# Another order for emptying two accumulator banks: VectorE leads with the first bank, ScalarE copies two parts instead of three

## The chip, the cores and the metric

The kernel runs on one core of one Trainium2 chip. The metric is the device time of one execution in microseconds; the time before is the median of three runs. A profiled execution comes with it: a trace of every instruction on the engines TensorE (PE), VectorE (DVE), ScalarE (ACT), GpSimd (POOL) and SyncE (SP).

## The reference

```python
# attention with a polynomial sketch, then an MLP with exact GELU
def phi(x):                       # x: (4, 4, 1088, 32)
    a = einsum('rd,bhsd->bhsr', S1, x)
    b = einsum('rd,bhsd->bhsr', S2, x)
    return einsum('bhsi,bhsj->bhsij', a, b).reshape(..., 64)
q_p, k_p = phi(q), phi(k)
kv = einsum('bhsf,bhsd->bhfd', k_p, v);  z = sum(k_p, axis=2)
attn = einsum('bhsf,bhfd->bhsd', q_p, kv) / (einsum('bhsf,bhf->bhs', q_p, z)[..., None] + 1e-6)
x = attn.transpose(0, 2, 1, 3).reshape(4352, 128)
h = x @ w_in                      # (4352, 2048)
g = 0.5 * h * (1 + erf(h / sqrt(2)))
out = g @ w_out                   # (4352, 128)
```

The second matrix product of the MLP, `g @ w_out`, is what the change touches, or rather the step that takes its results out of the accumulators.

## The kernel before

**Tiling.** The 4352 tokens are handled in nine chunks: n = 0 to 7 have 512 tokens each, n = 8 holds the 256 that are left over. `d_ff` = 2048 is cut into 16 slices of 128 (`fi`). One step of the main loop (line 1083) is one pair (n, fi): `hidden` (line 677) makes a 128x512 tile of h in a PSUM bank on TensorE (line 683), and ScalarE turns it into g with GELU (line 690).

**The second product in seven.** For chunks 2 to 7, and for the upper half of the slices of chunks 0 and 1, `g @ w_out` is done by a scheme of the Strassen kind: a 2x2 split of tokens, slices and output channels, with seven products in place of eight. GpSimd forms the sums of g (`token_sums`, lines 732 to 735), and of the weights (`channel_sums`). `two_products` (line 754, the matmul is line 767) issues the seven products two at a time, each in a 64-row half of one of two PSUM banks. `acc[n]` is the pair of banks (a0, a1) of chunk n. They come from the pool `ops`, which has two buffers, so a chunk takes over the very two banks of the chunk ahead of it. The table `PLACE` (line 706) says where each product lies: 1, 2, 3 and 5 in bank 0 (a0), 4, 6 and 7 in bank 1 (a1). The first products of a chunk are 4 and 7 (so they need a1), then 6; 1 and 5 follow (they need a0). The last products of a chunk are 2 and 3, in a0.

**The drain.** When the last product of a chunk is issued, the loop calls `drain(n)` (line 772), ahead of the next call of `hidden`. It takes the two banks out of PSUM into two tiles of SBUF, C and N, and forms on the way the partial sums of the scheme. Its lines:

- L779, L780, L781, all on ScalarE: copies of a1's upper half (64 rows x 512), of a quarter of a1 (64x256) and of a quarter of a0 (64x256, lower half, first columns, into N).
- L783 on VectorE: a1's lower half plus the copy of L779 (64x512). It is the last read of a1.
- L785 twice, L786, L787, L788 on VectorE: five additions of 64x256, each with one operand from a0. L788 adds the two column halves of a0's lower half: one of them from PSUM, the other from the copy that L781 made. It is the last read of a0.

Later `store(n)` combines C and N (lines 801 to 804), transposes (line 829) and writes the chunk out by SP's DMA queue (line 838 or 841).

**What sets the order.** Each engine runs its instructions in the order of the program text (lines 1133 to 1139 tie it down). Waits between engines are semaphores that the framework derives from the tiles that are read and written. The banks of the next chunk are free for TensorE once the last read of each is over.

Of the kernel before, what the change touches and what calls it, by code (L numbers as in the profile page):

```python
# [16 lines left out]
def kernel(  # L17
# [18 lines left out]
    pe, dve, act, pool, sp = nc.tensor, nc.vector, nc.scalar, nc.gpsimd, nc.sync  # L36
# [735 lines left out]
    def drain(n):  # L772


        C, N = (att.tile([128, 2, CW], FP, name="sums") for i in range(2))
        lo, hi, one, two = slice(0, 64), slice(64, 128), slice(0, HW), slice(HW, CW)
        a0, a1 = acc[n]

        act.copy(out=C[lo, 0], in_=a1[hi])  # L779
        act.copy(out=N[hi, 0, one], in_=a1[hi, one])  # L780
        act.copy(out=N[lo, 0, one], in_=a0[lo, one])  # L781

        dve.tensor_add(out=C[lo, 1], in0=a1[lo], in1=C[lo, 0])  # L783
        for half in (lo, hi):
            dve.tensor_add(out=C[half, 0, one], in0=a0[lo, one], in1=C[lo, 1, two])  # L785
        dve.tensor_add(out=C[hi, 0, two], in0=a0[hi, two], in1=C[hi, 0, one])  # L786
        dve.tensor_add(out=N[hi, 1, one], in0=a0[hi, one], in1=C[hi, 0, two])  # L787
        dve.tensor_add(out=N[lo, 1, one], in0=a0[lo, two], in1=N[lo, 0, one])  # L788
        drained[n] = C, N

    usual = {}
# [291 lines left out]
    for t in range(len(steps) + LAG):  # L1083
# [29 lines left out]
        for n in drains[t]:  # L1113
            drain(n)
# [55 lines left out]
```

## Time and profile before

| | us |
|---|---|
| median of three runs | 263.39 (263.13 to 263.56) |
| the profiled execution, its own time | 263.46 |
| its span, from first to last instruction | 261.7 |
| TensorE busy in the span | 256.7 |
| VectorE busy | 150.7 |
| ScalarE busy | 116.6 |
| GpSimd busy | 164.0 |

The granted TensorE clock is 1.000 over the span. "Chain of work" below means the chain that ended last, followed back from the last instruction; its list gives the start, the length and the kind of each piece. In the timeline a line gives start, duration, engine, source line, operation, output and input tiles, and in square brackets how long the engine sat idle ahead of it and what ended that. A matmul of fp32 data shows up as two entries of the trace; 64-column matmuls run two side by side, so two entries can carry the same start. The ends of matmuls are modelled.

There are eight drains (n = 0 to 7). Their L779 start at 67.11, 81.63, 109.79, 137.50, 166.41, 193.68, 221.31 and 245.83 us.

### The profile page before, as it was taken

How to read it: one execution, taken by the hardware profiler on the slowest of the kernel's cores; microseconds unless marked ns; L12 is line 12 of the kernel's file. 1: busy time of each engine (PE TensorE's matmuls, PEld its weight loads, DVE VectorE, ACT ScalarE, POOL GpSimd, SP SyncE). 2: the span in 40 equal slices, each digit the busy share in tenths (PEclk: the TensorE clock that was granted, in tenths of full speed). 3: DMA queues.
4: the chain of work that ended last, by engine and by line, in shares of the span. 5: the costliest groups of instructions: out<-in, count | busy, mean ns of one | idle time of the engine just before them, and what ended most of it. 6: DMA issues, size and time to landing. Idle time of an engine off the chain costs nothing.

```text
span 261.7 us, 5752 instructions
## 1 busy us (share of the span) xinstructions
PE 256.7 (98%) x2331; PEld 132.7 (51%) x2331; DVE 150.7 (58%) x307; ACT 116.6 (45%) x227; POOL 164.0 (63%) x173
## 2 busy tenths in 40 slices
PE   8999999999999999999999999999999999999994
PEld 6845444344444454444444454454444444445794
DVE  2885879969697997590267948450646042600240
ACT  4674767532635334533335334533362335334441
POOL 3403007799968767687758766967778676877200
PEclk9999999999999999999999999999999999999999
DMA  6469848831000101002000020010000100010020
GB/s 200 139 200 357 164 107 206 214 81 15 3 0 15 28 4 30 10 3 40 3 0 3 0 33 11 3 30 10 3 0 14 30 4 0 14 28 0 3 40 20
DMA packets 29530, 13.48 MB, mean 52 GB/s; under 512 B 21824, under 2 KB 27712, under 8 KB 29504
## 3 DMA queue, kind: packets, MB, share of 16 engines
q1 hardware_dynamic: 29472, 13.12, 20.5%
q8 instruction: 18, 0.29, 0.5%
q14 instruction: 8, 0.07, 0.1%
q10 hardware_dynamic: 32, 0.00, 0.0%
HBM read 10.88 MB, written 2.23 MB: 50 GB/s over the span
## 4 chain that ended last, share of the span: by engine, by line
PE 96%; DVE 1%; ACT 1%; issue 0%; DVEq 0%
PE h_ps L683 44%; PE o_ps L767 33%; PE o_ps L818 5%; PE w_ps L815 3%; PE w_ps L428 1%; PE w_ps L617 1%; PE w_ps L568 1%; PE w_ps L848 1%; PE h_ps L697 1%; PE o_ps L417 1%; PE h_ps L333 1%; PE w_ps L934 1%; PE w_ps L635 0%; PE w_ps L534 0%; DVE x_tok L656 0%
## 5 line engine op out<-in xcount | busy, mean ns | idle before, releaser
L683 PE MATMUL h_ps<-xT,w_in 128*64 128x512 f32 (+3 forms) x514 | 137.3, 576 | 0.0
L690 ACT ACTIVATE block<-h_ps 128x512 f32<-128x512 f32 (+1 forms) x128 | 73.0, 570 | 120.4 <-PE h_ps L683 114.6
L767 PE MATMUL o_ps<-block,w_out 128*64 128x256 f32 x224 | 57.9, 381 | 0.3 <-DVE sums L788 0.3
L683 PEld LDWEIGHTS h_ps<-xT,w_in 128*64 128x64 f32 (+1 forms) x514 | 41.8, 143 | 29.5 <-issue 11.6
L732 POOL TENSOR_TENSOR bits_low<-block 128x512 f32<-128x512 f32 x28 | 35.6, 1273 | 28.7 <-ACT block L690 28.7
L767 PEld LDWEIGHTS o_ps<-block,w_out 128*64 128x64 f32 x224 | 30.1, 137 | 39.3 <-issue 25.3
L733 POOL TENSOR_TENSOR bits_a<-block 128x512 f32<-128x512 f32 x28 | 35.7, 1276 | 13.4 <-ACT block L690 13.4
L734 POOL TENSOR_TENSOR bits_e<-bits_a,block 128x512 f32<-128x512 f32 x28 | 36.3, 1298 | 2.2
L735 POOL TENSOR_TENSOR bits_m<-block,bits_e 128x512 f32<-128x512 f32 x28 | 35.8, 1279 | 2.2
L767 PE MATMUL o_ps<-bits_low,small 128*64 128x256 f32 x112 | 29.3, 384 | 0.0
L767 PE MATMUL o_ps<-block,small 128*64 128x256 f32 x112 | 29.3, 384 | 0.0
L767 PE MATMUL o_ps<-bits_a,small 128*64 128x256 f32 x112 | 29.1, 383 | 0.0
L783 DVE TENSOR_TENSOR sums<-o_ps,sums 64x512 f32<-64x512 f32 x8 | 5.5, 682 | 41.1 <-ACT sums L780 23.6
L767 PE MATMUL o_ps<-bits_m,w_out 128*64 128x256 f32 x112 | 28.8, 380 | 0.0
L580 DVE STREAM_TRANSPOSE w_ps<-w_ps 128x512 f32<-128x512 f32 (+1 forms) x7 | 4.8, 691 | 38.8 <-PE w_ps L568 27.8
L767 PEld LDWEIGHTS o_ps<-block,small 128*64 128x64 f32 x112 | 14.5, 137 | 18.8 <-issue 9.1
L767 PE MATMUL o_ps<-bits_e,small 128*64 128x256 f32 x112 | 17.2, 385 | 0.0
L818 PE MATMUL o_ps<-g,w_out 128*128 128x512 f32 x32 | 16.4, 598 | 0.0
L767 PEld LDWEIGHTS o_ps<-bits_m,w_out 128*64 128x64 f32 x112 | 15.4, 137 | 0.0
L767 PEld LDWEIGHTS o_ps<-bits_a,small 128*64 128x64 f32 x112 | 14.7, 137 | 0.0
L767 PEld LDWEIGHTS o_ps<-bits_low,small 128*64 128x64 f32 x112 | 14.6, 137 | 0.0
L767 PEld LDWEIGHTS o_ps<-bits_e,small 128*64 128x64 f32 x112 | 7.5, 137 | 10.5 <-issue 9.1
(181 smaller groups left out, 300.6 us busy)
## 6 DMA issues: line engine op xcount, KB each, us to landing
out_dram<-oT SPq DMA_DIRECT2D x26, 64.0 KB, 2.2
block<-in_moe_w_in_dram SPq DMA_DIRECT2D x3, 512.0 KB, 7.4
block<-in_moe_w_out_dram SPq DMA_DIRECT2D x3, 512.0 KB, 12.7
k<-in_k_dram SPq DMA_DIRECT2D x12, 128.0 KB, 3.2
v<-in_v_dram SPq DMA_DIRECT2D x12, 128.0 KB, 3.4
q<-in_q_dram SPq DMA_DIRECT2D x24, 64.0 KB, 2.3
k<-in_k_dram SPq DMA_DIRECT2D x2, 256.0 KB, 2.9
q<-in_q_dram SPq DMA_DIRECT2D x2, 256.0 KB, 4.4
```

The source lines that it names most:

```text
L333: pe.transpose(ps[:, i * 128:(i + 1) * 128], in_=s, identity=ident)
L580: dve.transpose(out=tok, in_=ps[:, :, :H2])
L683: pe.matmul(ps[rows, :W], lhsT=w[:, rows], rhs=xT[n][:, :W], start=True, stop=True)
L690: act.activation(out=g_of[n, fi][:, :W], in_=ps[:, :W], func=ACT.Gelu)
L732: pool.tensor_sub(out=s[3], in0=a11, in1=a21)
L733: pool.tensor_add(out=s[1], in0=a21, in1=a22)
L734: pool.tensor_sub(out=s[2], in0=s[1], in1=a11)
L735: pool.tensor_sub(out=s[4], in0=a12, in1=s[2])
L767: pe.matmul(acc[n][bank][half * 64:(half + 1) * 64, col:col + HW], lhsT=fixed, rhs=moving, start=opens and e == 0 and name in "4715", stop ...
L783: dve.tensor_add(out=C[lo, 1], in0=a1[lo], in1=C[lo, 0])
L815: pe.matmul(o_of[n][i][:, :128], lhsT=g[:, i * 128:(i + 1) * 128], rhs=w_tile(w_out_sb, fi), start=first, stop=final)
L818: pe.matmul(o_of[n], lhsT=w_tile(w_out_sb, fi), rhs=g, start=first, stop=final)
```

## The change

The copy of a0's quarter (L781) goes from ScalarE to VectorE and to the head of VectorE's part of the drain; the addition that uses it (L788) goes from the tail of VectorE's part to the place right behind the copy. The other lines keep their order. ScalarE's part is L779 and L780 alone.

```diff
         act.copy(out=C[lo, 0], in_=a1[hi])
         act.copy(out=N[hi, 0, one], in_=a1[hi, one])
-        act.copy(out=N[lo, 0, one], in_=a0[lo, one])
-
+
+        dve.tensor_copy(out=N[lo, 0, one], in_=a0[lo, one])
+        dve.tensor_add(out=N[lo, 1, one], in0=a0[lo, two], in1=N[lo, 0, one])
         dve.tensor_add(out=C[lo, 1], in0=a1[lo], in1=C[lo, 0])
         for half in (lo, hi):
             dve.tensor_add(out=C[half, 0, one], in0=a0[lo, one], in1=C[lo, 1, two])
         dve.tensor_add(out=C[hi, 0, two], in0=a0[hi, two], in1=C[hi, 0, one])
         dve.tensor_add(out=N[hi, 1, one], in0=a0[hi, one], in1=C[hi, 0, two])
-        dve.tensor_add(out=N[lo, 1, one], in0=a0[lo, two], in1=N[lo, 0, one])
         drained[n] = C, N
```

## The prediction

> **What bounds the kernel now.** I read the page's busy times first, then the chain of work that ended last, then its pieces around one drain, then the timeline there, and last the list of waits. The page says that TensorE is the bound:
>
> ```profile
> PE 256.7 (98%) x2331; PEld 132.7 (51%) x2331; DVE 150.7 (58%) x307; ACT 116.6 (45%) x227; POOL 164.0 (63%) x173
> ...
> PE 96%; DVE 1%; ACT 1%; issue 0%; DVEq 0%
> ```
>
> The reader is to see that the chain is TensorE for 96%: another engine's time counts only where TensorE waits for it. The pieces of the chain around the drain of chunk 2 show that it does, a little, twice:
>
> ```profile
> 109.04 0.86 PE o_ps L767 x8
> 109.90 1.72 PE h_ps L683 x8
> 111.62 1.43 PE o_ps L767 x12
> 113.05 0.86 PE h_ps L683 x4
> 113.91 1.01 PE o_ps L767 x8
> ```
>
> Eight entries of L767 take 0.86 when nothing is in their way, so twelve should take 1.29. The piece at 111.62 has 1.43 (0.14 too much), the one at 113.91 has 1.01 (0.15 too much). The timeline of the same drain says why:
>
> ```profile
> 109.52 0.38 PE L767 MATMUL o_ps<-bits_m,w_out 128*64 128x256 f32 x1
> 109.73 1.89 PE L683 MATMUL h_ps<-xT,w_in 128*64 128x512 f32 x8
> 109.79 0.58 ACT L779 COPY sums<-o_ps 64x512 f32<-64x512 f32 x1
> ...
> 110.39 0.37 ACT L780 COPY sums<-o_ps 64x256 f32<-64x256 f32 x1
> ...
> 110.79 0.36 ACT L781 COPY sums<-o_ps 64x256 f32<-64x256 f32 x1
> 110.80 0.68 DVE L783 TENSOR_TENSOR sums<-o_ps,sums 64x512 f32<-64x512 f32 x1 [3.12 <-PE h_ps L683]
> ...
> 111.53 0.43 PE L767 MATMUL o_ps<-block,small 128*64 128x256 f32 x1
> ...
> 112.92 0.43 DVE L787 TENSOR_TENSOR sums<-o_ps,sums 64x256 f32<-64x256 f32 x1
> 113.37 0.42 DVE L788 TENSOR_TENSOR sums<-o_ps,sums 64x256 f32<-64x256 f32 x1
> ...
> 113.84 0.43 PE L767 MATMUL o_ps<-block,w_out 128*64 128x256 f32 x1
> ```
>
> L783 ends at 111.48, and the next chunk's first product on bank 1 starts 0.05 later; L788 ends at 113.79, and the first one on bank 0 starts 0.05 later. TensorE would have been there at 109.73 + 1.71 = 111.44 and at 112.88 + 0.86 = 113.74 (112.88 is L683's next start). L783 itself starts 0.04 after the end of L780, not of L779 whose data it adds, and VectorE has sat idle for 3.12 before it. The list of waits gives both, over all drains (total, times, longest):
>
> ```profile
> PEld o_ps L767 <- DVE sums L788: 5.2, 6, 1.2
> PEld o_ps L767 <- DVE sums L783: 4.7, 6, 0.8
> ```
>
> Those totals are idle time of the weight loads, which run ahead of the matmuls, so they overstate: what TensorE loses is the excess in the chain. That excess on bank 1 is 0.06 in drain 1 and 0.14 in drains 2, 3, 4 and 6; on bank 0 it is 0.15 in each of these. Drain 5 is special: VectorE's L785 starts 0.46 after L783's end (0.10 elsewhere), so L788 ends at 198.04; TensorE was due at 196.77 + 0.86 = 197.63, starts at 198.08, and its first pair takes 0.27 in place of 0.21: 0.51 lost. Drain 0 holds nobody (the next products on these banks start at 70.41, 1.6 after L783), nor does drain 7 (chunk 8 uses other banks).
>
> [...] L783 and L780 read different halves of a1, and still L783 waits L780 out. So VectorE can't touch a1 before about 110.80, but it can read a0 while ScalarE reads a1. [...] all eight L783 ran beside L781 and took 681 to 683 ns. [...] the trace's own row (L963, VectorE, 64x256 from a PSUM tile) has a mean of 420, which I use.
>
> **The change part by part.**
>
> *Removed from ScalarE:* L781, 0.37 x 8 = 2.9 us. It lay behind L780, and what follows it is L690, which starts at most 0.27 earlier. ScalarE has waited 0.5 to 1.7 for TensorE before most L690, so this gains nothing; without that cover it would be worth 0.27 a drain at the most. Nothing is moved past SP's or GpSimd's queue, and no DMA is issued in the drain.
>
> *Copy to VectorE, in front:* it needs a0's last product. In the built kernel of before L781 waits for the last product of the bank although it reads columns that an earlier one wrote, so I give the copy the same wait. The last pair starts at 109.52 and its modelled end is 109.90. What VectorE then needs to start isn't shown for this pair; L580 starts 0.11 after the modelled end of L568 in three chunks, 0.04 in a fourth. ScalarE's L690 needs 0.13 after L683. I take 0.11, bounds 0.04 and 0.13. Copy: 110.01 to 110.43. VectorE is idle then; nobody else is queued there but the drain.
>
> *Addition L788 moved behind the copy:* start 0.03 after (as L786 after L785), 0.42 long: 110.46 to 110.88.
>
> *L783:* it was let go at 110.80 by L780. It now comes behind the addition: 110.91 to 111.59, **0.11 later** (bounds 0.04 and 0.13; another 0.05 if the copy carries a second wait instruction). TensorE was already held by it, so the whole shift is paid: +0.11 in drains 2 to 6. In drain 1 ScalarE began earlier against TensorE: last product 81.44, so copy at 81.94, L783 at 81.94 + 0.90 = 82.84 against 82.64: +0.20.
>
> *The end of a0:* from L783's start on, 0.68 + 0.03 + 0.85 (two L785) + 0.03 + 0.43 + 0.03 + 0.43 = 2.48, so L787 ends at 113.39 and not L788 at 113.79. TensorE, itself 0.11 later, is due there at 113.85. The wait for a0 is gone, with 0.46 to spare: -0.15 in drains 1, 2, 3, 4, 6, and -0.51 in drain 5. Drain 5's odd gap of 0.36 may stay (L787 then ends at 194.80 + 2.48 + 0.36 = 197.64, TensorE is due at 197.74: still covered), or fall on another instruction (on L783 it would cost 0.36).
>
> *Sum:* drain 1 +0.20 - 0.15 = +0.05; drains 2, 3, 4, 6: 4 x (0.11 - 0.15) = -0.16; drain 5: 0.11 - 0.51 = -0.40. Together **-0.51 us**. Behind a drain nothing is late anew: VectorE is free 0.4 sooner, and work after it follows TensorE. Against the profiled execution's 263.46 this gives 262.95; that execution is 0.07 above the median, so on the median 262.9. What a measurement can tell from no change here is 0.2%, 0.53 us: the forecast lies just inside.
>
> **The rivals.** (a) *Slower: the new copy is held by ScalarE.* It writes into N, into which L780 writes as well. If the framework holds the copy until L780 has ended, copy and addition start at 110.80 and L783 at 111.70: +0.90 on bank 1 in six drains, 5.40 - (5 x 0.15 + 0.51 = 1.26) = +4.1: 267.5. It decides from a shift of 1.26 / 6 = 0.21 on; above 0.30 it is slower by more than 0.2%. Against it: L665 fills two halves of one tile from ScalarE and VectorE, and VectorE's half is released by TensorE alone; but those halves differ in columns, these in partitions. (b) *Nothing: the wait changes places.* If the start costs 0.05 more and the odd gap falls in front of L783, the sum is -0.51 + 0.30 + 0.36 = +0.15: 263.5. For it: the two effects are of one size. (c) *Earlier: the copy waits for product 1 alone*, and lies beside the last products. The addition then ends at 110.44, L783 keeps its time, and only the gain is left: -1.26, 262.1. Against it: L781's wait. That the change doesn't do what it says is (a).
>
> **How the numbers follow.** Forecast 0.62, with its own range 262.5 to 263.3 (0.11 replaced by 0.05 and 0.16, and the odd gap at either place); (a) 0.13, (b) 0.16, (c) 0.09. The forecast is split by its nearness to the bound: 0.28 faster, 0.34 within. Faster 0.28 + 0.09 = 0.37; within 0.2% 0.34 + 0.16 = 0.50; slower 0.13. Forecast and (b) hold 0.78, so the range takes in (c) as well: 262.0 to 263.7.
>
> **What would show it.** In the profile after: the copy starts about 0.1 after the last product's end and ahead of L780's end; L783 0.1 later against TensorE; the twelve-entry piece grows from 1.43 to about 1.54, the eight-entry piece falls from 1.01 to 0.86; no wait of L767 for a0's last addition. If the copy starts only behind L780, or the twelve-entry piece is over 1.64, the forecast is wrong; if L783 still starts 0.04 after L780's end, (c) is right.

## The result, and the profile after

The changed kernel takes 262.31 us (median of 11 runs, 261.74 to 262.94), the kernel before 263.6 in the same comparison (11 runs). The ratio is 0.9945, 95% interval 0.9928 to 0.9962: **faster by 1.45 us**, 1.0 to 1.9 by the interval. (The ratio is one of means; the medians differ by 1.29, because one run of the kernel before, at 265.31, lifts its mean.) The profiled execution has 261.87 us and a span of 260.1, 1.6 less than before.

In the changed kernel the drain's lines have other numbers: L779 and L780 are ScalarE's two copies, L782 the copy of a0's quarter on VectorE, L783 the moved addition, L784 the addition on bank 1 (L783 of before), L786 (twice), L787 and L788 the three lines after it (before: L785, L786, L787). L788 is now the last read of bank 0.

The page's busy times and the chain by engine:

```profile
PE 255.2 (98%) x2331; PEld 132.6 (51%) x2331; DVE 152.2 (59%) x315; ACT 114.6 (44%) x219; POOL 163.4 (63%) x173
...
PE 96%; DVE 1%; DMA 1%; ACT 1%; issue 0%; ACTq 0%; DVEq 0%
```

TensorE is still the bound. The piece of DMA in the chain, 1%, lies at the start, ahead of all drains. VectorE has eight instructions more and ScalarE eight fewer, as the diff says. The pieces of the chain around drain 2 (start, length, kind):

```profile
108.51 0.86 PE o_ps L767 x8
109.37 1.72 PE h_ps L683 x8
111.09 1.43 PE o_ps L767 x12
112.52 0.86 PE h_ps L683 x4
113.38 0.86 PE o_ps L767 x8
```

The eight-entry piece (four pairs with the same start to within 0.01, 0.21 to 0.22 from pair to pair) has fallen from 1.01 to 0.86, so the wait for bank 0 is gone. The twelve-entry piece is 1.43 as before: the wait for bank 1 hasn't grown. The timeline of the same drain:

```profile
109.00 0.38 PE L767 MATMUL o_ps<-bits_m,w_out 128*64 128x256 f32 x1
109.20 1.89 PE L683 MATMUL h_ps<-xT,w_in 128*64 128x512 f32 x8
109.26 0.58 ACT L779 COPY sums<-o_ps 64x512 f32<-64x512 f32 x1
...
109.42 0.42 DVE L782 COPY sums<-o_ps 64x256 f32<-64x256 f32 x1 [2.28 <-PE o_ps L767]
...
109.87 0.37 ACT L780 COPY sums<-o_ps 64x256 f32<-64x256 f32 x1
109.87 0.42 DVE L783 TENSOR_TENSOR sums<-o_ps,sums 64x256 f32<-64x256 f32 x1
...
110.27 0.68 DVE L784 TENSOR_TENSOR sums<-o_ps,sums 64x512 f32<-64x512 f32 x1
...
111.01 0.43 PE L767 MATMUL o_ps<-block,small 128*64 128x256 f32 x1
...
112.33 0.43 DVE L788 TENSOR_TENSOR sums<-o_ps,sums 64x256 f32<-64x256 f32 x1
...
113.21 0.38 PE L767 MATMUL o_ps<-block,w_out 128*64 128x256 f32 x1
```

Copy and moved addition lie in the time in which ScalarE holds bank 1. L784 starts 1.07 after TensorE's first L683 (110.27 - 109.20), exactly as L783 did before (110.80 - 109.73). L788 ends at 112.76, 0.45 before TensorE starts on bank 0; before, L788 ended 0.05 ahead of that start. In the list of waits the weight loads' wait for bank 0's last read has fallen from 5.2 to 1.9, that for bank 1 is 4.7 as it was:

```profile
PEld o_ps L767 <- DVE sums L784: 4.7, 6, 0.8
...
PEld o_ps L767 <- DVE sums L788: 1.9, 6, 0.3
```

And drain 5, where TensorE lost 0.51 before (0.15 as elsewhere and 0.36 through VectorE's odd gap), looks like the others (pieces of the chain):

```profile
192.82 1.72 PE h_ps L683 x8
194.54 1.43 PE o_ps L767 x12
195.97 0.86 PE h_ps L683 x4
196.83 0.86 PE o_ps L767 x8
```

**A yardstick.** The two spans differ by 1.6, but 0.39 of it lies ahead of the first drain: L779 of drain 0 starts at 67.11 before and at 66.72 after, and up to there the two kernels do the same. In the other profiles of this study that start lies anywhere from 66.7 to 68.9, in two profiles of the unchanged kernel at 67.11 and 67.42. So I read each profile from the start of L779 in drain 0 to its start in drain 7: 178.72 before, 177.49 after, **1.23 less**. The stalls account for that: six eight-entry pieces with 0.15 less (0.90) and drain 5's gap (0.36) make 1.26, and a twelve-entry piece in drain 1 that is 0.02 longer takes a little of it back.

### The profile page after: what moved, and what is told of

Read it like the earlier page. It is cut to its first block, busy times and chain, and to the rows that moved or that the text cites. A ratio compares the mean times of both kernels' runs of the same rounds, so it can differ in the third digit from the quotient of the medians.

```text
span 260.1 us, 5738 instructions
## 1 busy us (share of the span) xinstructions
PE 255.2 (98%) x2331; PEld 132.6 (51%) x2331; DVE 152.2 (59%) x315; ACT 114.6 (44%) x219; POOL 163.4 (63%) x173
## 4 chain that ended last, share of the span: by engine, by line
PE 96%; DVE 1%; DMA 1%; ACT 1%; issue 0%; ACTq 0%; DVEq 0%
PE h_ps L683 45%; PE o_ps L767 33%; PE o_ps L818 5%; PE w_ps L815 3%; PE w_ps L428 2%; PE w_ps L617 1%; PE w_ps L568 1%; PE h_ps L697 1%; DMA raw_SR<-in_S_dram 1%; PE o_ps L417 1%; PE w_ps L934 1%; PE w_ps L635 0%; PE w_ps L534 0%; DVE x_tok L656 0%; PE w_ps L333 0%; PE h_ps L635 0%
## 5 line engine op out<-in xcount | busy, mean ns | idle before, releaser
L683 PE MATMUL h_ps<-xT,w_in 128*64 128x512 f32 (+3 forms) x514 | 137.3, 576 | 0.0
L767 PE MATMUL o_ps<-block,w_out 128*64 128x256 f32 x224 | 57.5, 379 | 0.0
L683 PEld LDWEIGHTS h_ps<-xT,w_in 128*64 128x64 f32 (+1 forms) x514 | 41.8, 142 | 29.5 <-issue 11.6
L767 PEld LDWEIGHTS o_ps<-block,w_out 128*64 128x64 f32 x224 | 30.5, 137 | 37.5 <-issue 26.8
L767 PE MATMUL o_ps<-block,small 128*64 128x256 f32 x112 | 29.3, 384 | 0.0
L767 PE MATMUL o_ps<-bits_low,small 128*64 128x256 f32 x112 | 29.2, 384 | 0.0
L767 PE MATMUL o_ps<-bits_a,small 128*64 128x256 f32 x112 | 28.8, 379 | 0.0
L767 PE MATMUL o_ps<-bits_m,w_out 128*64 128x256 f32 x112 | 28.7, 379 | 0.0
L767 PEld LDWEIGHTS o_ps<-block,small 128*64 128x64 f32 x112 | 14.5, 136 | 18.9 <-issue 9.1
L782 DVE COPY sums<-o_ps 64x256 f32<-64x256 f32 x8 | 3.3, 417 | 34.7 <-PE o_ps L767 34.7
L767 PE MATMUL o_ps<-bits_e,small 128*64 128x256 f32 x112 | 17.1, 384 | 0.0
L767 PEld LDWEIGHTS o_ps<-bits_m,w_out 128*64 128x64 f32 x112 | 15.3, 137 | 0.0
L767 PEld LDWEIGHTS o_ps<-bits_a,small 128*64 128x64 f32 x112 | 15.2, 137 | 0.0
L767 PEld LDWEIGHTS o_ps<-bits_low,small 128*64 128x64 f32 x112 | 14.5, 137 | 0.0
L767 PEld LDWEIGHTS o_ps<-bits_e,small 128*64 128x64 f32 x112 | 7.5, 136 | 10.5 <-issue 9.1
```

The lines of the kernel that those rows point to most:

```text
L683: pe.matmul(ps[rows, :W], lhsT=w[:, rows], rhs=xT[n][:, :W], start=True, stop=True)
L767: pe.matmul(acc[n][bank][half * 64:(half + 1) * 64, col:col + HW], lhsT=fixed, rhs=moving, start=opens and e == 0 and name in "4715", stop ...
L782: dve.tensor_copy(out=N[lo, 0, one], in_=a0[lo, one])
```

## The experiments

| kernel | ratio to before (95%) | drain 0 to drain 7, us | less than before | pieces of twelve and eight |
|---|---|---|---|---|
| before | 1 | 178.72 | 0 | 1.43, 1.01 |
| changed | 0.9945 (0.9928 to 0.9962) | 177.49 | 1.23 | 1.43, 0.86 |
| copy alone | 0.9958 (0.9942 to 0.9975) | 177.97 | 0.75 | 1.43, 0.95 |
| addition alone | 0.9938 (0.9913 to 0.9962) | 177.47 | 1.25 | 1.43, 0.86 |
| ScalarE's load given back | 0.9943 (0.9922 to 0.9963) | 177.49 | 1.23 | 1.43, 0.86 |
| longer head | 0.9989 (0.9977 to 1.0001) | 178.44 | 0.28 | 1.51 behind a wait, 0.86 |
| two copies gone | 0.9915 (0.9892 to 0.9938) | 176.74 | 1.98 | 1.29, 0.86 |
| bank 1 with one reader | 0.9906 (0.9884 to 0.9929) | 176.76 | 1.96 | 1.29, 0.86 |
| the same, order as changed | 0.9953 (0.9938 to 0.9968) | 177.16 | 1.56 | 1.36, 0.86 |
| before, again | 0.999 (0.9975 to 1.0006) | 178.75 | -0.03 | 1.43, 1.02 |
| before, one more | 0.9988 (0.9969 to 1.0006) | 178.37 | 0.35 | 1.43, 1.01 |
| before, four more | 0.9988 (0.998 to 0.9995) | 178.37 | 0.35 | 1.43, 1.01 |

The stretch from drain to drain comes from one profile each; it and the timed ratios agree within the intervals. The diffs below are against the changed kernel, in the last two kernels against the kernel before.

My theory (A): TensorE loses only what the last reads of banks 1 and 0 end too late, and the change moves two operations into time in which VectorE was idle. The rivals were that ScalarE's relief pays (B), that the addition's place in VectorE's row pays (C), that what VectorE does ahead of the addition on bank 1 (its head) has time to spare (D, where the head is made longer; F, where ScalarE lets go of bank 1 sooner), and that the 0.14 left in the twelve-entry piece is no wait but TensorE's own switch from L683 to L767 (E).

**The copy alone on VectorE's head.** Of the change only the copy's move is kept; the addition is again the last of VectorE's part.

```diff
         dve.tensor_copy(out=N[lo, 0, one], in_=a0[lo, one])
-        dve.tensor_add(out=N[lo, 1, one], in0=a0[lo, two], in1=N[lo, 0, one])
         dve.tensor_add(out=C[lo, 1], in0=a1[lo], in1=C[lo, 0])
...
         dve.tensor_add(out=N[hi, 1, one], in0=a0[hi, one], in1=C[hi, 0, two])
+        dve.tensor_add(out=N[lo, 1, one], in0=a0[lo, two], in1=N[lo, 0, one])
```

> The copy of a0's quarter leads on VectorE as in the changed kernel and ScalarE has two copies, but the addition stays the last of VectorE's part. Theory A (only the moment at which bank 0 comes free counts): L783's place against TensorE as before, twelve-entry piece 1.43; the addition ends some 0.06 earlier than before, so the eight-entry piece falls only from 1.01 to about 0.95; with the odd gap of drain 5 gone 0.7 us faster than before, with it 0.35. Rival B (ScalarE's relief is what pays: GELU behind the drain starts 0.27 earlier): as fast as the changed kernel, 1.2 to 1.4 us faster than before, eight-entry piece 0.86.

Measured 0.75 less from drain to drain. VectorE in drain 2, and pieces of the chain in drain 5:

```profile
111.04 0.68 DVE L783 TENSOR_TENSOR sums<-o_ps,sums 64x512 f32<-64x512 f32 x1 [0.43 <-ACT sums L780]
111.76 0.85 DVE L785 TENSOR_TENSOR sums<-o_ps,sums 64x256 f32<-64x256 f32 x2
```

```profile
195.56 1.43 PE o_ps L767 x12
196.99 0.86 PE h_ps L683 x4
197.85 0.95 PE o_ps L767 x8
```

As theory A had it, in size too: some 0.06 a drain, and drain 5's gap gone. The 0.06 lie behind L783: L785 starts 0.04 after its end here and 0.10 after it in the kernel before. In the kernel before ScalarE reads bank 0 too, and VectorE's stream has one wait instruction of 0.02 ahead of each L785; the trace of the changed kernel has none ahead of L786, which starts 0.04 behind L784's end in drain 2. I take that instruction for the reason; no run changed it alone. ScalarE has two copies here as in the changed kernel, and the eight-entry piece still isn't 0.86, so B fails in the profile; the timed interval alone would not have told the two apart.

**The addition alone.** Of the change only the addition's move is kept, to the place behind the addition on bank 1; ScalarE has its three copies.

```diff
         act.copy(out=N[hi, 0, one], in_=a1[hi, one])
+        act.copy(out=N[lo, 0, one], in_=a0[lo, one])
...
-        dve.tensor_copy(out=N[lo, 0, one], in_=a0[lo, one])
-        dve.tensor_add(out=N[lo, 1, one], in0=a0[lo, two], in1=N[lo, 0, one])
         dve.tensor_add(out=C[lo, 1], in0=a1[lo], in1=C[lo, 0])
+        dve.tensor_add(out=N[lo, 1, one], in0=a0[lo, two], in1=N[lo, 0, one])
```

> ScalarE's three copies as before; of the change only the addition moves, to the place right behind the addition on bank 1 (L783 of before), where it finds its copy ready. Theory A (the gain is that two operations fill VectorE's idle time ahead of that addition): nothing is taken out of the stretch that ends with bank 0's last read, so the eight-entry piece stays at 0.95 to 1.01 and the time within 0.3 us of before, or 0.35 faster if drain 5's odd gap falls elsewhere. Rival C (that the addition is no longer last is what pays): 1.2 to 1.4 us faster, eight-entry piece 0.86.

Here my expectation failed: 1.25 less, as much as the whole change, and an eight-entry piece of 0.86. The first line is from drain 2 of the kernel before, the others are VectorE's timeline of drain 2 in this kernel:

```profile
111.58 0.85 DVE L785 TENSOR_TENSOR sums<-o_ps,sums 64x256 f32<-64x256 f32 x2
```

```profile
111.20 0.68 DVE L783 TENSOR_TENSOR sums<-o_ps,sums 64x512 f32<-64x512 f32 x1 [3.12 <-PE h_ps L683]
...
111.81 0.41 DVE L784 TENSOR_TENSOR sums<-o_ps,sums 64x256 f32<-64x256 f32 x1
...
112.14 0.84 DVE L786 TENSOR_TENSOR sums<-o_ps,sums 64x256 f32<-64x256 f32 x2
...
113.48 0.43 DVE L788 TENSOR_TENSOR sums<-o_ps,sums 64x256 f32<-64x256 f32 x1
```

From L783's start to the end of the last read it takes 113.91 - 111.20 = 2.71, against 113.79 - 110.80 = 2.99 before, with the same operations. Two things make up the 0.28 (to 0.01):

- Before, VectorE had to wait behind L783. L785 reads what L783 writes, and it started 0.78 behind L783's start (111.58 - 110.80). The moved addition (L784 here) doesn't read it and starts 0.61 behind, 0.07 ahead of L783's end: 0.17 of otherwise idle time is used.
- L786 then starts only 0.33 behind the addition. At the tail the addition itself had started 0.45 behind L787 (112.92 and 113.37 in the kernel before): 0.12 less.

For the second the traces show one thing that goes with it. In the old order the addition (lower half of the partitions) came behind L787 (upper half), 0.45 from start to start; in the new place L786 comes behind the addition, both on the lower half, and it is 0.33. In the x2 lines, too, the half changes: neither of the two operations reads the other's result, but the second writes the upper half, and two operations of 0.41 to 0.42 take 0.84 to 0.85 together, without overlap. That the half sets the distance is an estimate of mine from these three distances: no run changed the half alone.

So rival C is true beside A: the addition's place alone frees bank 0 by 0.28 sooner, and TensorE needed about 0.15. Theory A holds in that only the end of the last read counts. But the move to VectorE's head is one way to an earlier end, and not the only one: this kernel leaves the copy on ScalarE and gets as much.

**ScalarE's load given back.**

```diff
         act.copy(out=N[hi, 0, one], in_=a1[hi, one])
+        act.copy(out=N[lo, 1, two], in_=C[lo, 0, one])
```

> The changed kernel with a third copy of 64x256 given back to ScalarE behind its two: it copies values of C into a part of N that is written over later, so ScalarE has as much to do as before and VectorE's order is the changed one. Theory A: as the changed kernel, 1.2 to 1.4 us faster than before. Rival B (ScalarE's relief): as slow as before.

Measured: 177.49 from drain to drain (L779 starts at 67.57 in drain 0 and at 245.06 in drain 7), the same as the changed kernel. The third copy takes 0.40, no less than the one that was taken away. B falls: ScalarE's shorter part is worth nothing.

**A longer head.**

```diff
         dve.tensor_copy(out=N[lo, 0, one], in_=a0[lo, one])
+        dve.tensor_copy(out=N[lo, 1, two], in_=a0[lo, one])
```

> The changed kernel with the copy of a0's quarter made twice at VectorE's head (the second one into a part of N that is written over later). Theory A: VectorE's head just fits into the time in which ScalarE holds bank 1, so 0.45 more of it delays the addition on bank 1 by 0.45 in drains 1 to 6: twelve-entry piece 1.88, eight-entry piece 0.86, 2.7 us slower than the changed kernel and 1.4 slower than before. Rival D (the head starts so early, beside the last products, that it has time to spare): same as the changed kernel, 1.3 faster than before.

0.95 slower than the changed kernel from drain to drain, not 2.7. Direction as A, size a third. VectorE's part in drain 2, and the piece of the chain behind it:

```profile
109.96 0.42 DVE L782 COPY sums<-o_ps 64x256 f32<-64x256 f32 x1 [2.27 <-PE o_ps L767]
110.30 0.41 DVE L783 COPY sums<-o_ps 64x256 f32<-64x256 f32 x1
...
110.63 0.41 DVE L784 TENSOR_TENSOR sums<-o_ps,sums 64x256 f32<-64x256 f32 x1
...
110.96 0.67 DVE L785 TENSOR_TENSOR sums<-o_ps,sums 64x512 f32<-64x512 f32 x1
```

```profile
111.64 0.04 issue
111.69 1.51 PE o_ps L767 x12
```

The four starts are 0.34, 0.33 and 0.33 apart. With a second copy between, the addition no longer comes right behind the copy that it reads, so it needn't wait out 0.45; the head grows by 1.00 - 0.85 = 0.15 and not by 0.45. That 0.15 is paid: in drain 2 the stretch from the start of the eight-entry piece ahead (109.05) to the L683 behind the twelve (113.20) is 4.15, against 4.01 in the changed kernel. VectorE is on the chain now in each of drains 1 to 6. So the head had nothing to spare (D falls), but I had the price of one operation more wrong.

**What is left on bank 1.** If A is right, the 0.14 in the twelve-entry piece can be had too: ScalarE's second copy keeps VectorE off bank 1. Two kernels take it away.

Two copies gone:

```diff
         act.copy(out=C[lo, 0], in_=a1[hi])
-        act.copy(out=N[hi, 0, one], in_=a1[hi, one])
         dve.tensor_copy(out=N[lo, 0, one], in_=a0[lo, one])
-        dve.tensor_add(out=N[lo, 1, one], in0=a0[lo, two], in1=N[lo, 0, one])
         dve.tensor_add(out=C[lo, 1], in0=a1[lo], in1=C[lo, 0])
-        for half in (lo, hi):
-            dve.tensor_add(out=C[half, 0, one], in0=a0[lo, one], in1=C[lo, 1, two])
-        dve.tensor_add(out=C[hi, 0, two], in0=a0[hi, two], in1=C[hi, 0, one])
-        dve.tensor_add(out=N[hi, 1, one], in0=a0[hi, one], in1=C[hi, 0, two])
+        dve.tensor_add(out=N[lo, 1, one], in0=a0[lo, two], in1=N[lo, 0, one])
+        for half, to in ((lo, N), (hi, C)):
+            dve.tensor_add(out=to[half, 0, one], in0=a0[lo, one], in1=C[lo, 1, two])
+        dve.tensor_add(out=C[lo, 0, two], in0=a0[hi, two], in1=C[hi, 0, one])
+        dve.tensor_add(out=N[hi, 1, one], in0=a0[hi, one], in1=C[lo, 0, two])
...
-        dve.tensor_add(out=N[lo, 1, two], in0=C[lo, 1, one], in1=C[lo, 0, one])
-        dve.tensor_add(out=N[hi, 1, two], in0=N[hi, 0, one], in1=C[hi, 0, two])
+        dve.tensor_add(out=N[lo, 1, two], in0=C[lo, 1, one], in1=N[lo, 0, one])
+        dve.tensor_add(out=N[hi, 1, two], in0=C[lo, 0, one], in1=C[lo, 0, two])
```

> From the changed kernel: ScalarE's second copy out of bank 1 is gone too (its values are taken later from the copy that the first one made in C; two of the later additions write to other parts of C and N for that), and the addition on bank 1 comes ahead of the moved addition. Theory A (TensorE loses only what the last reads of banks 1 and 0 come too late, and bank 1 is held by ScalarE's second copy): the addition on bank 1 starts 0.67 after TensorE's first L683 behind the drain instead of 1.07; the twelve-entry piece falls from 1.43 to 1.29, the eight-entry piece stays at 0.86; 0.7 to 0.8 us faster than the changed kernel, 2.0 faster than before. Rival E (what is left in the twelve-entry piece is TensorE's own switch from L683 to L767, not a wait): 1.43 stays, as fast as the changed kernel.

Bank 1 with one reader on ScalarE's side:

```diff
-        act.copy(out=N[hi, 0, one], in_=a1[hi, one])
+        act.copy(out=N[hi, 0, one], in_=C[lo, 0, one])
         dve.tensor_copy(out=N[lo, 0, one], in_=a0[lo, one])
-        dve.tensor_add(out=N[lo, 1, one], in0=a0[lo, two], in1=N[lo, 0, one])
         dve.tensor_add(out=C[lo, 1], in0=a1[lo], in1=C[lo, 0])
+        dve.tensor_add(out=N[lo, 1, one], in0=a0[lo, two], in1=N[lo, 0, one])
```

> The same aim as in the kernel with two copies gone, by a smaller edit: ScalarE's second copy takes its values from C (SBUF) and not from bank 1, and the addition on bank 1 comes ahead of the moved addition. Theory A: bank 1's addition starts 0.67 after TensorE's first L683, twelve-entry piece 1.29, eight-entry piece 0.86, 2.0 us faster than before. Rival E: as the changed kernel, 1.3 faster than before.

Both came out as theory A said: 1.98 and 1.96 less than before. Timeline and chain of the second kernel in drain 2:

```profile
109.15 1.89 PE L683 MATMUL h_ps<-xT,w_in 128*64 128x512 f32 x8
109.21 0.58 ACT L779 COPY sums<-o_ps 64x512 f32<-64x512 f32 x1
...
109.82 0.68 DVE L783 TENSOR_TENSOR sums<-o_ps,sums 64x512 f32<-64x512 f32 x1
...
110.87 0.38 PE L767 MATMUL o_ps<-block,small 128*64 128x256 f32 x1
```

```profile
111.04 1.29 PE o_ps L767 x12
112.33 0.86 PE h_ps L683 x4
113.19 0.86 PE o_ps L767 x8
```

Bank 1's addition starts 0.67 behind TensorE's first L683 and ends at 110.50, 0.37 before TensorE is there; 1.29 is the length without a wait, so it was a wait and not TensorE's own switch (rival E falls). This kernel has the lowest time of the study: 261.23 us, ratio 0.9906 to the kernel before (0.9884 to 0.9929). Its interval and that of the kernel with two copies gone overlap, so which of the two is faster isn't known.

The same with the changed kernel's order on VectorE:

```diff
-        act.copy(out=N[hi, 0, one], in_=a1[hi, one])
+        act.copy(out=N[hi, 0, one], in_=C[lo, 0, one])
```

> ScalarE's second copy takes its values from C as in the run beside it, but VectorE keeps the changed kernel's order: copy, moved addition, addition on bank 1. Theory A: bank 1's addition is then held by VectorE's own head instead of by ScalarE. It can start 0.33 after the moved addition's start, 0.07 earlier than in the changed kernel: twelve-entry piece 1.36, 0.3 to 0.4 us faster than the changed kernel. Rival F (ScalarE's hold on bank 1 is the whole of it, the head has time to spare): twelve-entry piece 1.29, as fast as the run beside it.

```profile
112.05 0.42 DVE L783 TENSOR_TENSOR sums<-o_ps,sums 64x256 f32<-64x256 f32 x1
...
112.39 0.67 DVE L784 TENSOR_TENSOR sums<-o_ps,sums 64x512 f32<-64x512 f32 x1
```

```profile
113.27 1.36 PE o_ps L767 x12
```

The addition on bank 1 starts 0.34 behind the moved addition's start, the twelve-entry piece is 1.36, and the stretch 0.33 shorter than in the changed kernel: as expected, and F falls. In the changed kernel ScalarE's hold on bank 1 and VectorE's head end within 0.07 of each other; cutting ScalarE's alone gives 0.33, and for the whole 0.73 both have to be cut.

**The odd gap in drain 5.** It made up 0.36 of what the change saved, so I asked whether it belongs to the drain.

> The kernel of before, profiled once more. If the odd gap of 0.46 between L783 and L785 in drain 5 belongs to the program (to the place of the instruction), it is there again with an eight-entry piece of drain 5 that starts 0.45 late; if it is a chance event of that one execution, drain 5 looks like drains 2, 3, 4 and 6 (1.43 and 1.01), and the sum of the prediction holds 0.36 us that the change doesn't save in every run. The start up to the first drain: between the two profiles so far it differs by 0.39 us; by chance, if this profile's differs as well.

VectorE in drain 5 of the unchanged kernel, one line of the first profile and two of the second:

```profile
195.83 0.85 DVE L785 TENSOR_TENSOR sums<-o_ps,sums 64x256 f32<-64x256 f32 x2 [0.46 <-ACT block L690]
```

```profile
195.01 0.68 DVE L783 TENSOR_TENSOR sums<-o_ps,sums 64x512 f32<-64x512 f32 x1 [3.12 <-PE h_ps L683]
196.15 0.85 DVE L785 TENSOR_TENSOR sums<-o_ps,sums 64x256 f32<-64x256 f32 x2 [0.46 <-ACT block L690]
```

The gap is there again, in the same place and of the same length, so it isn't a chance event of one execution. Two kernels then put instructions on VectorE ahead of everything (`dve.memset(ones, 1.0)` once more, or four times more) and leave the drain as before:

```diff
     dve.memset(ones, 1.0)
+    dve.memset(ones, 1.0)
```

> The kernel of before with one more instruction on VectorE near its start (a tile of ones is set a second time), so that every later VectorE instruction has a place one further on in VectorE's stream. If the odd gap in drain 5 belongs to a place in the stream, it lies in front of the instruction ahead of L785 then (L783 or its wait), or is gone; drain 5's loss of 0.51 on bank 0 changes. If it belongs to the waits of that drain, it stays between L783 and L785 at 0.46.

> As the run beside it, with four more instructions in place of one: if the gap belongs to a place in VectorE's stream, it has left the drain (it would fall ahead of L783, where VectorE has idled for 3 us anyway), drain 5 looks like the other drains (1.43 and 1.01) and the kernel is 0.36 us faster than before. If it belongs to the waits of that drain, it stays at 0.46 between L783 and L785.

With one more, in drain 5 (lines are one higher):

```profile
194.94 0.68 DVE L784 TENSOR_TENSOR sums<-o_ps,sums 64x512 f32<-64x512 f32 x1 [3.12 <-PE h_ps L684]
195.73 0.85 DVE L786 TENSOR_TENSOR sums<-o_ps,sums 64x256 f32<-64x256 f32 x2
```

The gap is 0.11 now, with four more as well, and drain 5 has 1.43 and 1.01 in both. The waits of the drain are the same and the gap is gone, so it goes with a place in VectorE's stream and not with the drain's waits. By drain 5 the changed kernel has issued four VectorE instructions fewer (in a drain the copy is one more, and up to two wait instructions are gone: over the eight drains the trace of before has 16 ahead of L783 and L785, that of the changed kernel 2, ahead of L782 in drains 1 and 7), so the drain has moved against that place. What happens at that place wasn't found out. The timed ratios (0.9988 both) agree with 0.36 us, but only the second interval (0.998 to 0.9995) lies wholly below 1. Against these two kernels (178.37) the changed kernel is 0.88 shorter from drain to drain: that is what the new order is worth where the gap is away in both. The other 0.36 of the 1.23 came because the change shifted VectorE's stream.

## Why the prediction was right, and where it was off

The direction was right and the time lay in the range; the size was not: the forecast was 0.51 less, and the profile shows 1.23 less. 262.31 lies outside the forecast's own range (262.5 to 263.3). It is inside the stated one (262.0 to 263.7) only because that was drawn wide enough to take in rival (c), which had a chance of 0.09 and did not happen as it was told; so the number was hit in part by luck. The mechanism at bank 0 was right. Point by point:

- *What bounds the kernel, and where:* right. TensorE lost 0.15 at bank 0 and 0.14 at bank 1; the kernels that freed one or both got just these amounts back.
- *Bank 0's wait goes, with room to spare:* right. 0.15 in each of drains 1, 2, 3, 4 and 6 and 0.51 in drain 5, together -1.26, are all there. The room was predicted at 0.46 and is 0.45.
- *ScalarE's relief gains nothing:* right, shown by giving the load back.
- *L783 comes 0.11 later, +0.75 over six drains:* **this is the term that failed.** It measured 0.00 in drain 2, and at most 0.02 in drain 1, whose twelve-entry piece went from 1.35 to 1.37 where I had +0.20. Two sizes were wrong. First, the copy starts 0.04 behind the modelled end of the last product (109.00 + 0.38, then 109.42), the lower of my bounds, not 0.11: minus 0.07. (The 0.05 for a second wait instruction was an estimate; the copy had a wait instruction ahead of it in drains 1 and 7 alone, of 0.02.) Second, I let the addition on bank 1 wait for the end of the moved addition plus 0.03; it doesn't wait for that end (110.29) and starts at 110.27, 0.40 behind the moved addition's start: minus 0.05. Together 0.12, and the 0.11 is gone. What sets the start in drain 2 is L780 again, which ends at 110.24; without it, VectorE would go on 0.34 behind (as in the kernel with one reader and the changed order), so the second size was off by 0.11. In drain 1, where L780 ended earlier, all of that counts: 0.07 and 0.11 off the 0.20 leave the 0.02.
- *L783 waits for L780, which reads another half of a1:* the wait is in the trace (in drain 2 of before L783 starts 0.04 behind L780's end). Where L780 doesn't read the bank, L783 starts 0.03 behind L779's end (109.82 and 109.21 + 0.58, the kernel with one reader), so freeing the bank earlier pays. The wait is a semaphore that the framework derived; no run tried whether the halves could be read at once. Reads of different banks did run at once in the changed kernel: L782 on a0 (109.42 to 109.84) lies beside L779 on a1 (109.26 to 109.84), which took 0.58 as in the kernel before.
- *Drain 5's gap may stay or move:* it is gone from the drain. I had counted its 0.36 within bank 0's 0.51, as a gain of the new order. The amount was right, but it is one of the place in the stream: one extra instruction that changes no result gets it too. Had the gap stayed, the room of 0.45 would have been enough to cover it; that didn't come to a test.
- *Rivals:* (a) didn't happen: the copy starts 0.82 ahead of L780's end (110.24), though both write into N. (b) didn't happen. (c) gave the number, 1.26 less, but not by its mechanism: the copy is released by the bank's last product, not by product 1.

That the addition's place on VectorE is worth 0.28 by itself was in none of my cases. In the changed kernel it isn't needed, since the addition has left the stretch altogether.

## What to carry to other kernels

Where the bound engine waits for a buffer, look at the one read that ends last and let it end earlier: here two operations put into another engine's idle time took a wait of 0.15 off TensorE in each of six places, and moving one of them to where its engine would have waited anyway did the same. A stretch is only as movable as the next limit: ScalarE's hold on the bank and VectorE's own head ended within 0.07 of each other, and cutting the first alone gave 0.33 us, cutting both 0.73. When an operation is costed that follows another one on the same engine, take the distance from start to start for that pair, not the duration: for operations of 0.42 it was 0.33 or 0.34 where nothing held the second, and 0.45 where it was held. And where a profile has an odd gap, ask whether it stays when something unrelated is put ahead, before it is counted as a gain of the change.

## What the runs showed of the hardware that I had not expected

- VectorE started the next operation before the last had ended when it worked on the same half of the partitions and didn't wait for its result: 0.33 to 0.34 from start to start for 64x256 operations of 0.41 to 0.42; 0.45 where the half changed (L787 and L788 of before), and 0.45 where the second read the first one's result (L782 and L783 of the changed kernel).
- VectorE stood still for 0.36 longer than elsewhere at one place of its stream in two profiles of the kernel before; one instruction more ahead of it took that away. Its cause is open.
- A matmul that had to wait for its bank cost about 0.06 more than the wait: its first pair took 0.26 to 0.27 in place of 0.21, and its weight load started together with it and not ahead (before, drain 2: loads at 111.53 and 113.83, matmuls at 111.53 and 113.84). That the late load is the reason is likely, but not tested.
